# A gated mix of a segment-recurrent transformer and a gated MLP: the MLP branch and the output pass through DRAM scratches in segment and column-block order

## The chip, the cores and the metric

The kernel runs on one core of a Trainium2 chip. Its engines are TensorE (PE; its weight loads are listed as PEld), VectorE (DVE), ScalarE (ACT), GpSimd (POOL) and SyncE (SP). SP computes nothing here; it issues most of the DMAs, one after the other, and waits in its queue until the next one may start. Sixteen DMA engines carry the transfers. The metric is the device time of one execution, in microseconds.

## The reference

Two branches over the same kind of rows are mixed by a gate. Cut to what matters:

```python
# A: 64 segments of 32 rows, 8 memory rows carried from one to the next
for s in range(n_seg):                              # S = 2048 rows, Dm = 640
    h = concat([mem, x[:, 32*s : 32*s+32]], axis=1) # 40 rows
    q, k, v = (einsum('btd,dhe->bhte', h, W) for W in (Wq, Wk, Wv))   # 32 heads of 192
    p = softmax(where(mask, q @ k.T * 192**-0.5, -1e9))
    o = einsum('bhte,hed->btd', p @ v, Wo)
    mem = o[:, :8]; outs.append(o[:, 8:])
a = concat(outs, axis=1)
# B: a gated MLP, 640 -> 1536 -> 640
b = (gelu(x @ w_gate) * (x @ w_up)) @ w_down
g = sigmoid((x * gate_w).sum(-1, keepdims=True))
out = g * a + (1 - g) * b
```

The inputs are bfloat16, and so is the output of 2048 x 640.

## The kernel before

*The MLP first.* `ffn_gu` and `ffn_down` (lines 829 to 880) compute branch B in four blocks of 512 rows. `ffn_down` evacuates 128 rows at a time into a buffer `brow`, and one DMA from ACT's queue stores them into the DRAM tensor `ffn_b_scratch` (`b_scr`, line 878), row by row as the output has them.

*Then the chain of 64 segments* (`segment(s)`, line 1462). The weights Wq, Wk, Wv and Wo don't all fit in SBUF. Most pieces stay there; in each segment 13 pieces of Wq, Wk and Wv (384 KB each) and 3 of Wo (480 KB each) are swapped for their partners as soon as TensorE has used the old piece (`swap_loads`, `load_piece`, line 635). Segments run through the heads forwards and backwards in turn, so that the pieces used last are used first in the next one. What a segment does is a list written out by hand (`PROG`, `PROG1`, `PROG3`): groups of projections `("g", n, k)`, transposes, scores, softmax, `("pv", o)`, the output projection `("wo", o, half)`, and work for later segments (`lf`, `le`, `vb`) that fills TensorE's waits.

*The last 8 rows of a segment, called left rows,* don't feed the next segment's memory. Queries and keys of the left rows of four segments (a group, `g = s // 4`) are computed ahead together, and their output rows are projected with the last segment of the group (`wo_both`).

*The mix.* The output tile of a segment lies in SBUF as four column blocks of 160 on top of each other: partition 32 j + t holds row t, columns 160 j to 160 j + 159. The B rows must lie in the same way. `bz_load(s)` (line 1018) reads the 32 rows of segment s in that form from `ffn_b_scratch`; POOL scales them (`mix1`), DVE adds the gated A rows (`mix2`), and `out_store(s)` (line 1029) writes the tile to the output. The left rows of a group have a tile `bzl` of their own with 32 partitions for each column block, in the order: last segment of the group, then the other three (`LROW = ((3, 4), (0, 3))`). `bzl_load` (line 1024) fills it with eight DMAs, one of 8 and one of 24 rows for each column block; `outl_store` (line 1072) writes it out with eight.

*What sets the order.* Every instruction gets its semaphore waits from the regions that it reads and writes; within an engine, and within SP's queue, the order is the order of the calls. After the MLP all DMAs are issued by SP (`AUXQ = "sp"`, line 908). In a segment SP's queue holds: the K, Q and V pieces, each behind the TensorE instruction that frees its place; `out_store` of the segment before; the next segment's x rows; in the third segment of a group half of `bzl_load`, and in the first half of `outl_store`; the three Wo pieces; `bz_load`; the queries and keys of left rows (`stg_load`) around one more piece; and the other half of `bzl_load` or `outl_store`. The calls stand in the code as follows:

```python
if item == ("g", 1, KT - 1):
    if q:
        out_store(s - 1)
...
if item in (("g", 1, KT - 1), ("pv", NOCT - 2)):
    js = (0, 1) if item[0] == "g" else (2, 3)
    if q == 0 and g > 0:
        outl_store(g - 1, js)
    if q == 2 and g + 1 < NG:
        bzl_load(g, js)
```

*The end.* The last segment and the left rows of the last three are handled apart (`end_load`, `end_store`, line 1065), with six small transfers each from `ffn_b_scratch` and to the output.

Of the kernel before, what the change touches and what calls it, by code (L numbers as in the profile page):

```python
# [6 lines left out]
BF = mybir.dt.bfloat16  # L7
# [231 lines left out]
def _build(nc, A_x, A_mem0, A_Wq, A_Wk, A_Wv, A_Wo, seg_len, w_gate, w_up, w_down,  # L239
           gate_w, out, opts=None):  # L240
    opts = dict(opts or {})
    Bsz, S, Dm = A_x.shape
    M = A_mem0.shape[1]
    H, Dh = A_Wq.shape[1], A_Wq.shape[2]
    Df = w_gate.shape[1]
    L = int(seg_len)
    assert Bsz == 1 and M == 8 and L == 32 and Dh == 192
    assert Dm % 128 == 0 and H % 4 == 0 and S % 128 == 0 and Df % 128 == 0
    KT = Dm // 128
    DJ = Dm // 4  # L250
# [32 lines left out]
    g_scr = nc.dram_tensor("gate_scratch", (M, NSEG), F32, kind="Internal").ap()  # L283
# [163 lines left out]
    LROW = ((3, 4), (0, 3))  # L447
# [403 lines left out]
    def ffn_down(blk):  # L851
        n1 = min(Dm, 512)
        for a in range(FA):
# [14 lines left out]
            bs = a % NBR  # L868
# [18 lines left out]
    for blk in range(NFB):  # L887
        if blk:
            x_stage(blk)
        ffn_gu(blk)  # L890
        if blk == 0:
            chain_init()
        if blk + 1 < NFB:
            ffn_transposes(blk + 1)
        if blk + 2 < NFB:
            ffn_x_load(blk + 2)
        if blk + 1 == NFB:
            load_residents(1, lambda key: key not in loaded.values())
        ffn_down(blk)
        if blk + 2 == NFB:  # L900
            load_residents(1, lambda key: res_off[key] >= ffn_off["xr"] and res_off[key] + piece_size(key) <= ffn_off["xT"])
        if blk == 0:
            x_load(0)
            xl_load(0)
            xl_load(1)
            x_copy(0)
# [108 lines left out]
               name="Kl s%d o%d" % (s, o))  # L1015

    def bz_load(s):
        S_.add(AUXQ, lambda e: e.dma_start(bz, b_scr[L * s:L * s + L, :].rearrange("t (j n) -> j t n", j=4)),
               reads=[Rg("dr", 128 * (s // 4), 128 * (s // 4) + 128)], writes=[r_bz], dma_sem="bz", name="bz load s%d" % s)

    def bzl_load(g, js):
        for j in js:
            for n, (lo, hi) in enumerate(LROW):
                S_.add(AUXQ, lambda e, j=j, n=n, lo=lo, hi=hi: e.dma_start(
                    bzl[32 * j + M * n:32 * j + M * (n + hi - lo)], rows(b_scr, g)[1][lo:hi, :, DJ * j:DJ * (j + 1)]),
                    reads=[Rg("dr", 128 * g, 128 * g + 128)], writes=[r_bzlj[j][n]], dma_sem="bzl%d" % (2 * j + n), name="bzl load g%d" % g)

    def out_store(s):
        S_.add(AUXQ, lambda e: e.dma_start(out2[L * s:L * s + L, :].rearrange("t (j n) -> j t n", j=4), bz),
               reads=[r_bz], writes=[Rg("do%d" % j, s, s + 1) for j in range(4)], dma_sem="outs", watch=True, name="out s%d" % s)  # L1030

    assert r_XLg[1].lo == r_XLg[0].hi and KT * 64 == DJ * 2
    bzx = bview(wsA_off["XLg"], 4 * DJ)
# [4 lines left out]
    r_gx = sreg(wsA_off["xs"], 8)  # L1038

    def end_rows(ap, h, x, lo, hi):  # L1040
        v = ap[L * lo:L * hi, 2 * DJ * h:2 * DJ * (h + 1)]
        return v[0:XA] if x == 0 else v.rearrange("(s t) d -> s t d", t=L)[:, XA:L, :]

    def end_load():
# [21 lines left out]
                   reads=[r_bzx[i]], writes=[Rg("do%d" % (2 * h + t), lo, hi, *((XA, L) if x else (0, XA))) for t in range(2)],  # L1066
                   dma_sem="outx%d" % i, watch=True, name="out end")

    def outl_store(g, js):
        for j in js:  # L1070
            for n, (lo, hi) in enumerate(LROW):
                S_.add(AUXQ, lambda e, j=j, n=n, lo=lo, hi=hi: e.dma_start(
                    rows(out2, g)[1][lo:hi, :, DJ * j:DJ * (j + 1)], bzl[32 * j + M * n:32 * j + M * (n + hi - lo)]),
                    reads=[r_bzlj[j][n]], writes=[Rg("do%d" % j, 4 * g + lo, 4 * g + hi)], dma_sem="outl%d" % (2 * j + n), watch=True, name="outl g%d" % g)

    omg = fview(wsA_off["stats"] + 64, 8)
    r_omg = sreg(wsA_off["stats"] + 64, 8)
# [384 lines left out]
    def segment(s):  # L1462
# [3 lines left out]
        for n, item in enumerate(PROGS[q]):  # L1466
# [210 lines left out]
```

## Time and profile before

| | |
|---|---|
| median of three runs | 1651.54 us (1647.38 to 1653.57) |
| profiled execution, span | 2114.2 us |
| granted TensorE clock in it | 0.654 |
| busy share PE, DVE, ACT, POOL | 99%, 48%, 38%, 26% |
| DMA, mean over the span | 236 GB/s, 499.28 MB in 275415 packets |

The profiled execution is the one that the hardware profiler recorded, from its first to its last instruction; it is longer than the timed runs, and its granted clock stands beside it. A matmul's end is modelled, so a TensorE that is busy all the time need not be at its peak. "SPq" is SP's queue; its instructions take time to issue but aren't counted as busy. A DMA row shows how many transfers of a kind were issued, their size, and the median time from issue to landing where that could be found. The DMA share of a stretch is the mean over sixteen engines.

### The profile page before, as it was taken

What the parts mean: (1) busy time and instruction counts of PE and PEld (TensorE: products, weight loads), DVE (VectorE), ACT (ScalarE), POOL (GpSimd) and SP (SyncE); (2) the same over time, 40 slices, a digit from 0 to 9 for tenths busy, and PEclk for the clock granted to TensorE, in tenths of its full rate; (3) what the DMA queues carried; (4) which work ended last, traced back from release to release, by engine and by line L of the source; (5) the groups of instructions that cost most, each with busy time, mean ns of one, the idle gap of its engine ahead of it and who ended that gap; (6) DMA issues with size and microseconds to landing.
All of it is one profiled execution on the core that took longest, in us unless ns stands there. A gap on an engine that the chain in (4) does not pass through costs nothing.

```text
span 2114.2 us, 75845 instructions
## 1 busy us (share of the span) xinstructions
PE 2098.0 (99%) x37107; PEld 958.1 (45%) x28147; DVE 1005.8 (48%) x3039; ACT 792.9 (38%) x1890; POOL 553.3 (26%) x1625
## 2 busy tenths in 40 slices
PE   9999999999999999999999999999999999999997
PEld 3444344444444444444444444444444444444444
DVE  4233254554545454545545454545455454545453
ACT  1111244343434343444434343434444343434342
POOL 1000023232232223232222323232322223222332
PEclk6666666666666666666666666666666666666666
DMA  9612577776768777677767677776777676777775
GB/s 319 182 33 57 184 268 260 248 270 232 253 219 275 244 258 241 227 255 254 274 233 249 221 268 249 255 251 225 248 256 270 239 258 212 261 256 249 254 264 174
DMA packets 275415, 499.28 MB, mean 236 GB/s; under 512 B 121119, under 2 KB 136327, under 8 KB 275079
## 3 DMA queue, kind: packets, MB, share of 16 engines
q1 hardware_dynamic: 271000, 491.30, 68.8%
q8 instruction: 255, 4.18, 0.8%
q10 hardware_dynamic: 4079, 3.14, 0.5%
q14 instruction: 81, 0.66, 0.1%
HBM read 473.25 MB, written 21.09 MB: 234 GB/s over the span
## 4 chain that ended last, share of the span: by engine, by line
PE 99%; DMA 0%; DVE 0%; SPq 0%; POOL 0%; ACT 0%; issue 0%; ACTq 0%; POOLq 0%; DVEq 0%
PE ps L226 26%; PE ps L1138 25%; PE ps L1338 9%; PE ps L1383 8%; PE ps L1282 4%; PE ps L930 4%; PE ps L839 4%; PE ps L836 4%; PE ps L862 3%; PE ps L1364 3%; PE ps L1187 2%; PE ps L1284 2%; PE ps L234 1%; PE ps L1195 1%; PE ps L971 1%; PE ps L1254 1%
## 5 line engine op out<-in xcount | busy, mean ns | idle before, releaser
L226 PE MATMUL ps<-arena 128*32 128x384 bf16 x8960 | 887.8, 430 | 0.4 <-ACT arena L1159 0.4
L1138 PE MATMUL ps<-arena 128*32 128x384 bf16 x8640 | 857.5, 420 | 2.0 <-DVE arena L1583 2.0
L1138 PEld LDWEIGHTS ps<-arena 128*32 128x32 bf16 x8640 | 303.3, 117 | 525.3 <-issue 379.7
L1176 DVE STREAM_TRANSPOSE arena<-arena 128x384 bf16<-128x384 bf16 x512 | 276.5, 562 | 144.1 <-ACT arena L1159 144.1
L1159 ACT ACTIVATE arena<-ps 128x384 bf16<-128x384 f32 x512 | 230.0, 491 | 160.1 <-PE ps L1138 160.1
L1214 DVE TENSOR_REDUCE arena<-ps 104x4 f32<-104x160 f32 x256 | 83.0, 324 | 340.2 <-PE ps L1202 340.2
L1338 PE MATMUL ps<-arena 128*32 128x320 bf16 x3456 | 241.0, 404 | 0.0
L1012 POOL COPY arena<-arena 128x96 bf16<-128x96 bf16 x256 | 70.2, 274 | 475.3 <-PE ps L1202 311.4
L1267 ACT ACTIVATE arena<-ps 128x448 bf16<-128x448 f32 x192 | 104.4, 544 | 237.7 <-PE ps L1254 233.3
L1179 POOL COPY arena<-arena 64x160 bf16<-64x160 bf16 x256 | 81.9, 320 | 385.5 <-DVE arena L1176 384.3
L1162 ACT ACTIVATE arena<-ps 128x384 bf16<-128x384 f32 x256 | 125.2, 489 | 128.1 <-PE ps L1138 127.5
L1383 PE MATMUL ps<-arena 128*64 128x320 bf16 x1536 | 169.6, 387 | 0.0
L1226 ACT ACTIVATE ps<-ps 104x160 f32<-104x160 f32 x256 | 74.8, 292 | 239.5 <-DVE ps L1216 239.5
L1320 ACT ACTIVATE arena<-ps 128x480 bf16<-128x480 f32 x192 | 109.5, 570 | 93.8 <-PE ps L1284 85.7
L930 PE MATMUL ps<-arena 128*32 128x384 bf16 x1280 | 142.5, 408 | 0.0
L1338 PEld LDWEIGHTS ps<-arena 128*32 128x32 bf16 x3456 | 113.3, 129 | 56.9 <-ACT arena L1261 18.1
L1282 PE MATMUL ps<-arena 128*64 128x160 bf16 x1536 | 135.2, 263 | 0.0
L1284 PE MATMUL ps<-arena 128*64 128x64 bf16 x1536 | 128.6, 225 | 0.0
L1228 DVE TENSOR_REDUCE arena<-ps 104x4 f32<-104x160 f32 x256 | 81.8, 319 | 88.4 <-ACT ps L1226 87.4
L1383 PEld LDWEIGHTS ps<-arena 128*64 128x64 bf16 x1536 | 93.2, 127 | 49.4 <-issue 9.6
L1282 PEld LDWEIGHTS ps<-arena 128*64 128x64 bf16 x1536 | 94.1, 126 | 42.8 <-ACT arena L1159 23.0
L1411 ACT ACTIVATE arena<-ps 128x384 bf16<-128x384 f32 x120 | 57.3, 491 | 123.9 <-DVE arena L1580 74.0
(102 smaller groups left out, 2518.2 us busy)
## 6 DMA issues: line engine op xcount, KB each, us to landing
arena<-in_A_Wk_dram SPq DMA_DIRECT2D x335, 384.0 KB, 5.8
arena<-in_A_Wv_dram SPq DMA_DIRECT2D x335, 384.0 KB, 8.4
arena<-in_A_Wo_dram SPq DMA_DIRECT2D x205, 480.0 KB, 4.3
arena<-in_A_Wq_dram SPq DMA_DIRECT2D x209, 384.0 KB, 4.8
arena<-left_qk_scratch SPq DMA_DIRECT2D x126, 96.0 KB, 3.9
left_qk_scratch<-arena SPq DMA_DIRECT2D x49, 192.0 KB, 4.6
left_qk_scratch<-arena SPq DMA_DIRECT2D x30, 96.0 KB, 3.7
ffn_b_scratch<-arena ACTq DMA_DIRECT2D x16, 160.0 KB, 2.3
```

Source lines behind the costliest of these rows:

```text
L226: return e.add_instruction(mybir.InstMatmult(name=nm, start_tensor_calc=like["start"], stop_tensor_calc=stop, tile_size=(128, 32), tile_po ...
L930: fns.append(lambda e, outp=outp, rhs=rhs, j=j: e.matmul(outp, lhs, rhs, start=(k == 0), stop=(k == KT - 1), tile_position=(0, 32 * j)))
L1138: fns.append(lambda e, outp=outp, rhs=rhs, j=j: e.matmul(outp, lhs, rhs, start=(k == 0), stop=(k == KT - 1), tile_position=(0, 32 * j)))
L1159: S_.add("act", lambda e, m=m, bk=bk: e.activation(out=rows_sb[m], in_=ps[:, bk, 0:384], func=ACTF.Copy), reads=[r_ps[bk]], writes=[r_rows ...
L1162: S_.add("act", lambda e, i=i, bk=bk: e.activation(out=v_sb[i % NVB].rearrange("p (c n) -> p c n", c=3), in_=ps[:, bk, 0:384].rearrange("p ...
L1176: S_.add("dve", lambda e: e.transpose(out=dst[:, :, 0:L], in_=rows_sb[m].rearrange("p (c r) -> p c r", r=L)), reads=[r_rows[m]], writes=[r ...
L1267: S_.add("act", lambda e: e.activation(out=PT, in_=ps[:, bank, 0:PTW + 128], func=ACTF.Copy), reads=[r_ps[bank]], writes=[r_PT], name="pT ...
L1282: return [lambda e: e.matmul(full, v[:, e0:e0 + 64], PTm[:, i], start=True, stop=False, tile_position=(0, 64 * i), skip_group_check=True), ...
L1284: lambda e: e.matmul(part, vl[:, e0:e0 + 64], PTl[:, i], start=False, stop=True, tile_position=(0, 64 * i), skip_group_check=True)]
L1320: S_.add("act", lambda e: e.activation(out=apx(u[:, 0, 0, :], [[rs, na], [3 * rs, 4], [1, R]]), in_=ps[:, A, 0:na * W].rearrange("p (c t r ...
L1338: fns.append(lambda e, i=i, t=t, j=j, gv=gv: e.matmul(ps[32 * j:32 * j + 32, bank, 0:2 * DJ].rearrange("p (h n) -> p h n", h=2), lhs2[i], ...
L1383: S_.add("pe", [lambda e, i=i, g_=g_, c=c, p=p, u=u: e.matmul(ps[64 * i:64 * i + 64, LB, 0:2 * DJ], u[:, c, :], g_[:, c, 2 * DJ * i:2 * DJ ...
```

## The change

Five things are done:

1. The B rows are stored by `ffn_down` into a scratch `b_segments` whose order is segment, column block, row, column. Each 128 rows take four DMAs (one a segment) instead of one; for the last of the four blocks SP issues them instead of ACT. Only the last 128 rows also go to `ffn_b_scratch`, for the end.
2. `bz_load` reads 40 KB that lie in one piece in DRAM, as 128 rows of 160, and `out_store` writes such a piece into a scratch `out_segments` (segments 0 to 59). The last segments still write to the output.
3. The left rows of B are copied, DRAM to DRAM, from `b_segments` into a scratch `b_left` in the order of the tile `bzl` (`b_left_copy`: four during the MLP for the first half of the segments, four during segments 3 to 6 for the second). `bzl_load` and `outl_store` are one DMA each, from `b_left` and to `out_left`.
4. When sixteen segments are finished, the left rows are copied from `out_left` to their places in `out_segments` (`out_left`, four DMAs, one in each of the first four segments after that), and then `out_segments` to the output (`out_copy`, four DMAs, one for each column block, in the four segments that follow). Segments 48 to 59 are copied in segments 61 and 62, four DMAs in each.
5. The places of the calls: `outl_store` stands where its first half stood, `bzl_load` where its second half stood; the copies stand behind `stg_load` in the turn to the next segment.

The diff, without the renamed lines of the end:

```diff
-    b_scr = nc.dram_tensor("ffn_b_scratch", (S, Dm), BF, kind="Internal").ap()
+    b_scr = nc.dram_tensor("ffn_b_scratch", (128, Dm), BF, kind="Internal").ap()
+    b2_scr, o2_scr = [nc.dram_tensor(nm, (NSEG, 4, L, Dm // 4), BF, kind="Internal").ap() for nm in ("b_segments", "out_segments")]
+    b3_scr, o3_scr = [nc.dram_tensor(nm, (NG, 4, 4, M * (Dm // 4)), BF, kind="Internal").ap() for nm in ("b_left", "out_left")]
...
-            S_.add(AUXQ, lambda e, bs=bs, row0=row0: e.dma_start(b_scr[row0:row0 + 128, :], brow[bs]),
-                   reads=[r_brow[bs]], writes=[Rg("dr", row0, row0 + 128)], dma_sem="bw%d" % bs, watch=True,
-                   name="b store %d" % row0)
+            for q in range(4):
+                S_.add("sp" if blk + 1 == NFB else AUXQ, lambda e, bs=bs, row0=row0, q=q: e.dma_start(
+                    b2_scr[row0 // L + q].rearrange("j t n -> t j n"), brow[bs][L * q:L * q + L].rearrange("t (j n) -> t j n", j=4)),
+                    reads=[r_brow[bs]], writes=[Rg("d2", row0 // L + q, row0 // L + q + 1)], dma_sem="bw%d_%d" % (bs, q),
+                    name="b store %d" % row0)
+            if row0 + 128 == S:
+                S_.add("sp", lambda e, bs=bs: e.dma_start(b_scr, brow[bs]), reads=[r_brow[bs]], writes=[Rg("dr", S - 128, S)],
+                       dma_sem="bwl", name="b store")
+
+    def seg_left(scr, lo, hi, q):
+        return scr[lo:hi].rearrange("(g q) j t n -> q g j (t n)", q=4)[q][:, :, XA * DJ:L * DJ]
+
+    def b_left_copy(half, q):
+        g0, g1 = 8 * half, 8 * half + 8
+        S_.add("sp", lambda e: e.dma_start(b3_scr[g0:g1, :, (q + 1) % 4], seg_left(b2_scr, 4 * g0, 4 * g1, q)),
+               reads=[Rg("d2", 4 * g0, 4 * g1)], writes=[Rg("d3", 4 * half + q, 4 * half + q + 1)],
+               dma_sem="bl%d" % q, name="b left copy %d %d" % (half, q))
...
+        if blk == 2:
+            for q in range(4):
+                b_left_copy(0, q)
...
     def bz_load(s):
-        S_.add(AUXQ, lambda e: e.dma_start(bz, b_scr[L * s:L * s + L, :].rearrange("t (j n) -> j t n", j=4)),
-               reads=[Rg("dr", 128 * (s // 4), 128 * (s // 4) + 128)], writes=[r_bz], dma_sem="bz", name="bz load s%d" % s)
-
-    def bzl_load(g, js):
-        for j in js:
-            for n, (lo, hi) in enumerate(LROW):
-                S_.add(AUXQ, lambda e, j=j, n=n, lo=lo, hi=hi: e.dma_start(
-                    bzl[32 * j + M * n:32 * j + M * (n + hi - lo)], rows(b_scr, g)[1][lo:hi, :, DJ * j:DJ * (j + 1)]),
-                    reads=[Rg("dr", 128 * g, 128 * g + 128)], writes=[r_bzlj[j][n]], dma_sem="bzl%d" % (2 * j + n), name="bzl load g%d" % g)
+        S_.add(AUXQ, lambda e: e.dma_start(bz, b2_scr[s].rearrange("j t n -> (j t) n")),
+               reads=[Rg("d2", s, s + 1)], writes=[r_bz], dma_sem="bz", name="bz load s%d" % s)
+
+    def bzl_load(g):
+        S_.add(AUXQ, lambda e: e.dma_start(bzl, b3_scr[g].rearrange("j q (t n) -> (j q t) n", n=DJ)),
+               reads=[Rg("d3", 4 * (g // 8), 4 * (g // 8) + 4)], writes=[r_bzl], dma_sem="bzl", name="bzl load g%d" % g)
 
     def out_store(s):
+        if s < NSEG - 4:
+            S_.add(AUXQ, lambda e: e.dma_start(o2_scr[s].rearrange("j t n -> (j t) n"), bz), reads=[r_bz],
+                   writes=[Rg("o2", s, s + 1)], dma_sem="outs", name="out s%d" % s)
+            return
         S_.add(AUXQ, lambda e: e.dma_start(out2[L * s:L * s + L, :].rearrange("t (j n) -> j t n", j=4), bz),
...
-    def outl_store(g, js):
...
+    def outl_store(g):
+        S_.add(AUXQ, lambda e: e.dma_start(o3_scr[g].rearrange("j q (t n) -> (j q t) n", n=DJ), bzl), reads=[r_bzl],
+               writes=[Rg("o3", g, g + 1)], dma_sem="outl", name="outl g%d" % g)
+
+    def out_left(lo, hi, q):
+        g0, g1 = lo // 4, hi // 4
+        form = "g j x -> g j x" if g1 - g0 == 4 else "g j x -> j g x"
+        S_.add(AUXQ, lambda e: e.dma_start(seg_left(o2_scr, lo, hi, q).rearrange(form), o3_scr[g0:g1, :, (q + 1) % 4].rearrange(form)),
+               reads=[Rg("o3", g0, g1)], writes=[Rg("o2", lo, hi)], dma_sem="outf%d" % q, name="out left s%d" % lo)
+
+    def out_copy(lo, hi, j):
+        form = "s t n -> s t n" if hi - lo == 16 else "s t n -> t s n"
+        S_.add(AUXQ, lambda e: e.dma_start(
+            out2[L * lo:L * hi, DJ * j:DJ * (j + 1)].rearrange("(s t) n -> s t n", t=L).rearrange(form),
+            o2_scr[lo:hi].rearrange("s j t n -> j s t n")[j].rearrange(form)),
+            reads=[Rg("o2", lo, hi)], writes=[Rg("do%d" % j, lo, hi)], dma_sem="outm%d" % j, watch=True, name="out copy s%d" % lo)
...
                     stg_load(s + 1, int(q != 1))
+                if 3 <= s <= 6:
+                    b_left_copy(1, s - 3)
+                lo, i = s // 16 * 16 - 16, s % 16 - 1
+                if lo >= 0 and 0 <= i < 8:
+                    (out_left if i < 4 else out_copy)(lo, lo + 16, i % 4)
+                if s in (NSEG - 3, NSEG - 2):
+                    for i in range(4):
+                        (out_left if s == NSEG - 3 else out_copy)(NSEG - 16, NSEG - 4, i)
...
-            if item in (("g", 1, KT - 1), ("pv", NOCT - 2)):
-                js = (0, 1) if item[0] == "g" else (2, 3)
-                if q == 0 and g > 0:
-                    outl_store(g - 1, js)
-                if q == 2 and g + 1 < NG:
-                    bzl_load(g, js)
+            if item == ("g", 1, KT - 1) and q == 0 and g > 0:
+                outl_store(g - 1)
+            if item == ("pv", NOCT - 2) and q == 2 and g + 1 < NG:
+                bzl_load(g)
```

More of the change, by code (lines that the diff above doesn't have):

```diff
@@ L1017, in bz_load @@
     def bz_load(s):
-        S_.add(AUXQ, lambda e: e.dma_start(bz, b_scr[L * s:L * s + L, :].rearrange("t (j n) -> j t n", j=4)),
-               reads=[Rg("dr", 128 * (s // 4), 128 * (s // 4) + 128)], writes=[r_bz], dma_sem="bz", name="bz load s%d" % s)
-    def bzl_load(g, js):
-        for j in js:
-            for n, (lo, hi) in enumerate(LROW):
-                S_.add(AUXQ, lambda e, j=j, n=n, lo=lo, hi=hi: e.dma_start(
-                    bzl[32 * j + M * n:32 * j + M * (n + hi - lo)], rows(b_scr, g)[1][lo:hi, :, DJ * j:DJ * (j + 1)]),
-                    reads=[Rg("dr", 128 * g, 128 * g + 128)], writes=[r_bzlj[j][n]], dma_sem="bzl%d" % (2 * j + n), name="bzl load g%d" % g)
+        S_.add(AUXQ, lambda e: e.dma_start(bz, b2_scr[s].rearrange("j t n -> (j t) n")),
[3 more added lines that the diff above has]
+               reads=[Rg("d3", 4 * (g // 8), 4 * (g // 8) + 4)], writes=[r_bzl], dma_sem="bzl", name="bzl load g%d" % g)
     def out_store(s):
+        if s < NSEG - 4:
+            S_.add(AUXQ, lambda e: e.dma_start(o2_scr[s].rearrange("j t n -> (j t) n"), bz), reads=[r_bz],
+                   writes=[Rg("o2", s, s + 1)], dma_sem="outs", name="out s%d" % s)
+            return
         S_.add(AUXQ, lambda e: e.dma_start(out2[L * s:L * s + L, :].rearrange("t (j n) -> j t n", j=4), bz),
-               reads=[r_bz], writes=[Rg("do%d" % j, s, s + 1) for j in range(4)], dma_sem="outs", watch=True, name="out s%d" % s)
+               reads=[r_bz], writes=[Rg("do%d" % j, s, s + 1) for j in range(4)], dma_sem="oute", watch=True, name="out s%d" % s)
     assert r_XLg[1].lo == r_XLg[0].hi and KT * 64 == DJ * 2
@@ L1040, in end_rows @@
     def end_rows(ap, h, x, lo, hi):
-        v = ap[L * lo:L * hi, 2 * DJ * h:2 * DJ * (h + 1)]
+        off = S - ap.shape[0]
+        v = ap[L * lo - off:L * hi - off, 2 * DJ * h:2 * DJ * (h + 1)]
         return v[0:XA] if x == 0 else v.rearrange("(s t) d -> s t d", t=L)[:, XA:L, :]
@@ L1067, in end_store @@
                    dma_sem="outx%d" % i, watch=True, name="out end")
-    def outl_store(g, js):
[L1070 to L1074, printed above, removed]
+    def outl_store(g):
[12 more added lines that the diff above has]
+            reads=[Rg("o2", lo, hi)], writes=[Rg("do%d" % j, lo, hi)], dma_sem="outm%d" % j, watch=True, name="out copy s%d" % lo)
     omg = fview(wsA_off["stats"] + 64, 8)
```

## The prediction

> **What bounds the kernel now.** I read first the page's head with the cores' list, then the stages, then the DMA issues, last SP's queue in one segment.
>
> ```profile
> core 0: 2114.2 us, clock 0.654
> ```
>
> ```profile
> PE 2098.0 (99%) x37107; PEld 958.1 (45%) x28147; DVE 1005.8 (48%) x3039; ACT 792.9 (38%) x1890; POOL 553.3 (26%) x1625
> ...
> DMA packets 275415, 499.28 MB, mean 236 GB/s; under 512 B 121119, under 2 KB 136327, under 8 KB 275079
> ...
> q1 hardware_dynamic: 271000, 491.30, 68.8%
> ...
> q10 hardware_dynamic: 4079, 3.14, 0.5%
> ...
> PE 99%; DMA 0%; DVE 0%; SPq 0%; POOL 0%; ACT 0%; issue 0%; ACTq 0%; POOLq 0%; DVEq 0%
> ```
>
> The profiled execution is TensorE alone: 99% busy, 99% of the chain that ended last. If that were all, a change of transfers would be worth nothing. But this execution ran at a granted clock of 0.654 and took 2114.2 us, while the three timed runs have a median of 1651.54, which is 0.781 of it. So the timed runs had a faster TensorE, and what hides behind it in the profile need not be hidden in them. At full clock its work would be 2098.0 x 0.654 = 1372 us; 280 us of the median are then something else. The other reading is that TensorE is still the bound, at a clock of 0.654 / 0.781 = 0.84. The stages decide between them (columns: busy time of PE, PEld, DVE, ACT, POOL with counts, granted clock, DMA share, GB/s):
>
> ```profile
> 0.00:242.40 242.40, 240.38 (x882) 98.46 (x883) 80.42 (x144) 39.24 (x66) 16.65 (x39) 0.66 0.50 145
> 242.40:279.20 36.80, 36.45 (x672) 14.24 (x470) 17.24 (x49) 14.60 (x33) 7.90 (x24) 0.65 0.86 312
> 279.20:2069.10 1789.90, 1787.76 (x34988) 828.87 (x26348) 894.38 (x2800) 727.13 (x1763) 519.56 (x1534) 0.65 0.73 249
> 2069.10:2114.20 45.10, 33.39 (x580) 16.53 (x452) 13.80 (x46) 11.88 (x30) 9.20 (x29) 0.63 0.46 157
> ```
>
> The third row is 62 segments: 28.9 us each, of which the sixteen DMA engines are busy 0.73 x 28.9 = 21.1 us in the mean. TensorE needs 28.8 us at 0.654, so 18.9 at full clock: less than the DMA engines. The other rows at full clock: 159 us (TensorE, first row), 0.86 x 36.8 = 32 (DMA, second), 33.4 x 0.654 + 11.7 idle = 34 (last). Together 225, which leaves (1651.5 - 225) / 62 = 23.0 us for a segment of the timed runs, if they ran at full clock. TensorE's 18.9 doesn't explain that; the DMA mean of 21.1 nearly does.
>
> What is above the mean? The issues (out<-in, engine, count, KB each, median us to landing):
>
> ```profile
> arena<-in_A_Wo_dram SPq DMA_DIRECT2D x205, 480.0 KB, 4.3
> arena<-in_A_Wq_dram SPq DMA_DIRECT2D x209, 384.0 KB, 4.8
> ...
> left_qk_scratch<-arena SPq DMA_DIRECT2D x49, 192.0 KB, 4.6
> left_qk_scratch<-arena SPq DMA_DIRECT2D x30, 96.0 KB, 3.7
> ...
> arena<-ffn_b_scratch SPq DMA_DIRECT2D x63, 40.0 KB
> out_dram<-arena SPq DMA_DIRECT2D x63, 40.0 KB
> ...
> arena<-ffn_b_scratch SPq DMA_DIRECT2D x60, 2.5 KB
> arena<-ffn_b_scratch SPq DMA_DIRECT2D x60, 7.5 KB
> out_dram<-arena SPq DMA_DIRECT2D x60, 2.5 KB
> out_dram<-arena SPq DMA_DIRECT2D x60, 7.5 KB
> ```
>
> The view gives a landing time only where completions of all sixteen engines are found. The rows without one are just those whose pattern's outermost dimension is small: 4 (column blocks) for the 40 KB ones, 8 and 3 for the left rows. I read them as running on 4, 8 and 3 engines.
>
> **The price of a row.** All these transfers move rows of 320 B. The stretch in which only weight loads run gives the rate of an engine:
>
> ```profile
> 870.00:878.00 8.00, 0.65 1.03 409
> ```
>
> 409 / 16 = 25.6 GB/s, so 320 B cost at least 12.5 ns. From the other side, the ACT queue (q10) took 0.5% of 16 x 2114.2 us for 4079 packets of 770 B in the mean, 41 ns each. I take 27 ns, the middle. Rows on the busiest engines in a group of four segments: 4 x 32 (bz load) + 4 x 32 (out store) + left rows, load and store, 2 x (4 x 8 + 4) = 328, that is 82 a segment or 2.2 us; the mean over sixteen engines is 20 rows, 0.54 us. The busiest thus hold 21.1 + 1.7 = 22.8 us of work in a segment, against the 23.0 above. I conclude that the timed runs are held by three or four overloaded DMA engines.
>
> **The change, part by part.** One segment (third of four) of SP's queue:
>
> ```profile
> 899.70 1.38 SPq L635 DMA_DIRECT2D arena<-in_A_Wv_dram  x3
> 901.12 0.60 SPq L1029 DMA_DIRECT2D out_dram<-arena  x1
> 901.76 0.47 SPq L743 DMA_DIRECT2D arena<-x_scratch  x1
> 902.28 2.84 SPq L1024 DMA_DIRECT2D arena<-ffn_b_scratch  x4
> 910.18 2.81 SPq L635 DMA_DIRECT2D arena<-in_A_Wo_dram  x3
> 913.04 0.59 SPq L1018 DMA_DIRECT2D arena<-ffn_b_scratch  x1
> 913.67 0.48 SPq L1005 DMA_DIRECT2D arena<-left_qk_scratch  x1
> 914.67 0.33 SPq L635 DMA_DIRECT2D arena<-in_A_Wq_dram  x1
> 915.04 0.44 SPq L1005 DMA_DIRECT2D arena<-left_qk_scratch  x1
> 915.53 2.38 SPq L1024 DMA_DIRECT2D arena<-ffn_b_scratch  x4
> 920.72 2.11 SPq L635 DMA_DIRECT2D arena<-in_A_Wk_dram  x2
> ```
>
> *Out store, L1029.* 32 rows on four engines become 8 on sixteen: 24 x 27 = 0.65 us less there, 0.22 more elsewhere. It stands between the Wv loads and the Wo loads, which TensorE needs next, so it is on the path.
> *Left rows, L1024 and L1072.* 72 rows a group become 16: 14 a segment, 0.38 us. Half stands ahead of the Wo loads (0.2 us on the path), half in the turn of the segment. SP issues 14 fewer in a group; the four at 902.28 took 2.84 us, but SP then waited until 910.18 for TensorE. At full clock the 9.1 us from 901.12 shrink to 5.9 and SP's issues there take 0.60 + 0.47 + 2.84 = 3.9: still covered, so nothing for it.
> *bz load, L1018.* Also 0.65 us less, but in the turn: from 913.04 to 920.72 SP only waits for TensorE to give the K slots back, 7.7 us, about 5 at full clock. There the queue holds bz, two of L1005, one Wq load (384 KB, 0.96 us at 409 GB/s). It counts where that backlog still stands when the Wk loads come; half of it, 0.3 us.
> *Added: copies of the output inside DRAM.* Every finished sixteen segments get four out_left copies (rows of 2560 B, with the same for the b rows 0.5 row or 0.05 us a segment and engine) and four out_copy of 512 rows of 320 B, so 8 rows a segment and engine, 60 segments. No row shows a DRAM to DRAM transfer. Lower bound 12.5 ns, above; the 512-row stores (L1419, 96 KB, 3.7 us to landing) land no later than the 128-row ones of 192 KB (4.6), so such 32 rows an engine cost under 1 us, 31 ns. I take the dearer 41 ns: 0.33 us a segment. They are issued in the turn, behind the Wq load, four segments in sixteen, 1.3 us each, and wait for stores a segment old. No cover is left there if the engines are the bound, so it counts in full.
> *FFN.* The b rows are stored in four parts by segment. For three blocks ACT issues them; it is busy 39.24 of 242.40 us, so it hides there. In the last block SP issues 16 and one for the end, each behind an evacuation; the resident Wo loads are next in that queue, and five issues of 0.6 us put them 3 us later in a stage bound by DMA: +3 us once.
> *End.* In segment 61 the four last out_left wait for one another, three landings of some 3.7 us (the 96 KB stores' row), 11 us, less the 5 that the turn covers, and the Wk loads stand behind them: +6 us once (0 to 11).
>
> Were every engine's work the whole time, a segment would go from 22.8 to 21.1 - 0.54 + 0.54 + 0.33 + 0.05 = 21.5 us: 1.3 us, 81 us over 62. That is the high end. By the path alone it is 0.65 + 0.2 + 0.3 - 0.38 = 0.77. I take 0.85, nearer the path: 53 us, less 9 once: 1651.5 - 44 = **1607 us**. Against the profile's own time: at 0.654 TensorE covers all of it, and I expect its span within 2100 to 2120 if the clock is the same.
>
> **Rivals.**
> *TensorE bounds the timed runs, at 0.84 (no change).* For it: 1372 / 0.84 + 16 = 1649. Against it: the DMA's 22.8 us would be longer than 18.9 / 0.84 = 22.5, so even then the engines take part. It gives 1645 to 1658.
> [...]
> *Turn-bound (small gain).* If the waits at the turn (last Wo load, sums, K slots, new loads) set the period, only 0.3 us a segment are won: 1651 - 19 + 9 = 1641.
> *Dear copies (slower).* A row read from DRAM and written to DRAM, 320 B at a time into a pitch of 1280 B, may cost far more than a row to or from SBUF. 480 of them lie on every engine; from 41 + 44000 / 480 = 133 ns on, the change loses; at 200 ns it gives 1607 + 480 x 0.159 = 1683. Against it: the 512-row store above.
> [...]
> *It doesn't do what it says.* If the 40 KB transfers ran on sixteen engines already, only the copies remain: 0.38 x 60 + 9 = 32 us more, 1683. The missing landing times speak against it.
>
> **How the numbers follow.** Overloaded engines 0.55 (1565 to 1633), turn-bound 0.15 (1633 to 1643 for the most part), TensorE 0.10, dear copies 0.14, no effect 0.06. About 0.5% (8 us) is what can be told from no change. Faster 0.70, same 0.10, slower 0.20. The range runs from 1562 (the high end of 81 us and no cost of the end) to 1662 (just above the no-change case); it leaves out the slower cases.
>
> **What would show it.** Right: the 40 KB rows and the single left transfer have landing times, four rows of copies appear, and the runs are about 44 us faster though the profiled span hardly moves. Copies: landing near 4 us and a DMA share that rises by about 0.01; near 8 us and more, they are dear. Wrong: no gain with all that in place would mean that the overloaded engines were not the bound; a loss, that the copies or SP's waits in front of the Wk loads are.

## The result, and the profile after

| | median | ratio to before |
|---|---|---|
| before | 1651.54 us (1646.53 to 1659.29, 11 runs) | |
| after | 1663.57 us (1656.38 to 1670.41, 11 runs) | 1.0077 (95%: 1.0057 to 1.0098) |

The change costs 12.7 us (0.0077 x 1651.5). Forecast were 1607 us, in a range of 1562 to 1662. The profiled execution of after ran at a clock of 0.994; so the kernel before was profiled once more, and that execution ran at 0.995. These two can be compared row by row, which the record at 0.654 didn't allow; they differ by 9.1 us. First the cores' list and rows 1 and 3 of the page, for before:

```profile
core 0: 1652.2 us, clock 0.995
...
PE 1565.1 (95%) x37090; PEld 776.7 (47%) x28147; DVE 997.8 (60%) x3039; ACT 784.5 (47%) x1890; POOL 549.6 (33%) x1625
...
q1 hardware_dynamic: 271000, 491.30, 84.8%
```

and for after:

```profile
core 0: 1661.3 us, clock 0.994
...
PE 1570.3 (95%) x37107; PEld 774.2 (47%) x28147; DVE 999.9 (60%) x3039; ACT 785.2 (47%) x1890; POOL 551.9 (33%) x1625
...
q1 hardware_dynamic: 282644, 495.85, 85.7%
```

TensorE is busy 95% of either span, and SP's queue q1 puts 0.857 x 1661.3 - 0.848 x 1652.2 = 23 us more work on each DMA engine. Now the stages. I cut them at the end of the MLP and at two starts of POOL's copy of the next segment's x rows (line 811 before, 813 after), which comes once a segment; between its starts for segments 1 and 63 lie 62 segments. Columns as in the prediction. Before:

```profile
0.00:168.00 168.00, 162.16 (x870) 78.90 (x887) 82.37 (x144) 39.12 (x66) 16.22 (x39) 0.99 0.71 209
168.00:195.60 27.60, 25.94 (x673) 11.52 (x472) 17.09 (x49) 14.52 (x32) 7.85 (x24) 1.00 0.97 357
195.60:1612.00 1416.40, 1351.24 (x34988) 671.88 (x26348) 884.35 (x2800) 719.05 (x1763) 516.39 (x1533) 1.00 0.89 316
1612.00:1652.20 40.20, 25.72 (x580) 14.40 (x451) 14.02 (x48) 11.77 (x30) 9.18 (x29) 0.87 0.50 180
```

After, with a fifth row for the last of the 62:

```profile
0.00:170.40 170.40, 163.58 (x887) 78.17 (x887) 82.49 (x144) 38.92 (x66) 15.84 (x39) 1.00 0.74 207
170.40:201.30 30.90, 27.56 (x666) 11.51 (x458) 17.31 (x49) 14.67 (x33) 7.93 (x25) 0.94 0.86 307
201.30:1622.00 1420.70, 1354.08 (x34992) 670.27 (x26358) 886.43 (x2801) 719.85 (x1763) 518.88 (x1534) 1.00 0.90 317
1622.00:1661.30 39.30, 25.08 (x580) 14.22 (x448) 13.64 (x46) 11.71 (x30) 9.21 (x29) 0.91 0.58 195
1592.40:1622.00 29.60, 21.92 (x508) 9.59 (x380) 12.81 (x42) 10.20 (x26) 8.01 (x25) 0.88 0.75 261
```

A segment takes 1416.40 / 62 = 22.84 us before and 1420.70 / 62 = 22.91 after; without the last one 1391.1 / 61 = 22.80. So the segments gain next to nothing, and the loss sits in two places: the MLP and what follows it up to segment 1 (2.4 + 3.3 us), and one segment near the end, 29.6 us instead of 23.1 (1612.0 - 1588.9, POOL's last two of these copies before). It runs from the copy for segment 62 to that for 63; the transfers that delay it are issued in segment 61, and the texts below call it segment 61.

The DMA issues of after show that the change does what it says:

```profile
arena<-b_segments SPq DMA_DIRECT2D x63, 40.0 KB, 4.6
out_segments<-arena SPq DMA_DIRECT2D x60, 40.0 KB, 9.1
...
out_dram<-out_segments SPq DMA_DIRECT2D x12, 160.0 KB, 4.4
...
arena<-b_left SPq DMA_DIRECT2D x15, 40.0 KB, 3.3
out_left<-arena SPq DMA_DIRECT2D x15, 40.0 KB, 8.6
...
out_segments<-out_left SPq DMA_DIRECT2D x12, 40.0 KB
```

The 40 KB transfers between SBUF and the scratches now have landing times, which the view gives only where it finds sixteen completions for each. The 63 loads from `b_segments` have 1008 in the trace; the 63 from `ffn_b_scratch` before had 315, five each. The copies to the output land in 4.4 us. The copies of left rows (last line) have no landing time and five completions each, so by the prediction's reading they still run on fewer engines. "On four engines" is that reading in the texts below too: no trace here names the engine that a row ran on.

### The profile page after: what moved, and what is told of

Same layout as the page of the kernel before. It is cut to its first block, busy times and chain, and to the rows that moved or that the text cites. A ratio compares the mean times of both kernels' runs of the same rounds, so it can differ in the third digit from the quotient of the medians.

```text
span 1661.3 us, 75708 instructions
## 1 busy us (share of the span) xinstructions
PE 1570.3 (95%) x37107; PEld 774.2 (47%) x28147; DVE 999.9 (60%) x3039; ACT 785.2 (47%) x1890; POOL 551.9 (33%) x1625
## 3 DMA queue, kind: packets, MB, share of 16 engines
q10 hardware_dynamic: 8687, 2.49, 0.7%
## 5 line engine op out<-in xcount | busy, mean ns | idle before, releaser
L1169 PE MATMUL ps<-arena 128*32 128x384 bf16 x8640 | 642.7, 329 | 19.9 <-DMA arena<-in_A_Wv_dram 7.8
L226 PE MATMUL ps<-arena 128*32 128x384 bf16 x8960 | 646.8, 327 | 5.0 <-DMA arena<-in_A_Wq_dram 1.2
L1169 PEld LDWEIGHTS ps<-arena 128*32 128x32 bf16 x8640 | 227.2, 96 | 396.1 <-issue 263.4
L1369 PE MATMUL ps<-arena 128*32 128x320 bf16 x3456 | 184.1, 301 | 12.0 <-issue 6.8
L1031 POOL COPY arena<-arena 128x96 bf16<-128x96 bf16 x256 | 69.6, 272 | 246.2 <-PE ps L1233 158.2
L1313 PE MATMUL ps<-arena 128*64 128x160 bf16 x1536 | 118.1, 240 | 5.8 <-ACT arena L1190 3.4
L1414 PE MATMUL ps<-arena 128*64 128x320 bf16 x1536 | 122.3, 304 | 0.9 <-DMA arena<-in_A_Wo_dram 0.6
L1369 PEld LDWEIGHTS ps<-arena 128*32 128x32 bf16 x3456 | 88.2, 96 | 54.7 <-ACT arena L1292 18.6
L949 PE MATMUL ps<-arena 128*32 128x384 bf16 x1280 | 108.9, 329 | 0.9 <-issue 0.9
L1315 PE MATMUL ps<-arena 128*64 128x64 bf16 x1536 | 104.1, 193 | 1.3 <-issue 1.3
L1359 POOL COPY arena<-arena 128x96 bf16<-128x96 bf16 x192 | 51.7, 269 | 160.6 <-ACT arena L1341 93.8
L1313 PEld LDWEIGHTS ps<-arena 128*64 128x64 bf16 x1536 | 81.7, 109 | 41.2 <-ACT arena L1193 14.4
```

Of the source, the lines that this page charges most:

```text
L226: return e.add_instruction(mybir.InstMatmult(name=nm, start_tensor_calc=like["start"], stop_tensor_calc=stop, tile_size=(128, 32), tile_po ...
L949: fns.append(lambda e, outp=outp, rhs=rhs, j=j: e.matmul(outp, lhs, rhs, start=(k == 0), stop=(k == KT - 1), tile_position=(0, 32 * j)))
L1169: fns.append(lambda e, outp=outp, rhs=rhs, j=j: e.matmul(outp, lhs, rhs, start=(k == 0), stop=(k == KT - 1), tile_position=(0, 32 * j)))
L1313: return [lambda e: e.matmul(full, v[:, e0:e0 + 64], PTm[:, i], start=True, stop=False, tile_position=(0, 64 * i), skip_group_check=True), ...
L1315: lambda e: e.matmul(part, vl[:, e0:e0 + 64], PTl[:, i], start=False, stop=True, tile_position=(0, 64 * i), skip_group_check=True)]
L1369: fns.append(lambda e, i=i, t=t, j=j, gv=gv: e.matmul(ps[32 * j:32 * j + 32, bank, 0:2 * DJ].rearrange("p (h n) -> p h n", h=2), lhs2[i], ...
```

## The experiments

Effects in microseconds are (ratio - 1) x 1651.5, and each trace is of one execution. Theory 1 and 2 are those of the expectations.

**The kernel before once more** (no edit).

> The kernel before, unchanged, for a profile at the clock of the timed runs. Theory 1 (the overloaded engines never set the pace; the change only pays waits at single places, at the end of the MLP and in segment 61): segments of 22.9 us as in the changed kernel, within 0.1, and segment 61 near 22 us instead of 29.6. Theory 2 (the spreading gains, but the copies inside DRAM cost more): segments of 22.7, of equal length in every block of sixteen, while those of the changed kernel are longer where copies are issued.

Median 1648.89 us, ratio 0.9991 (0.996 to 1.0023). The profiled execution took 1653.96 us at a clock of 0.995; its rows stand above. TensorE is busy 1351.24 / 62 = 21.8 us in a segment of 22.84. That is theory 1, but for the 23.1 us of segment 61.

**Three parts of the change.** Without the copies of finished segments (the output of segments 0 to 59 then stays in the scratch):

```diff
-                if lo >= 0 and 0 <= i < 8:
-                    (out_left if i < 4 else out_copy)(lo, lo + 16, i % 4)
-                if s in (NSEG - 3, NSEG - 2):
...
```

> The changed kernel without out_left and out_copy: segments 0 to 59 never reach the output, which is left out here. Theory 1: only the wait in segment 61 goes, about 7 us, so 1656. Theory 2: the copies' whole price goes and the gain of the sixteen engines is seen: 1620 to 1635.

Only the way of the B rows (items 1, half of 2 and half of 3 of the change), with `out_store` and `outl_store` as before:

```diff
     def out_store(s):
-        if s < NSEG - 4:
-            S_.add(AUXQ, lambda e: e.dma_start(o2_scr[s].rearrange("j t n -> (j t) n"), bz), reads=[r_bz],
...
```

> The kernel before with the change's B side alone (b_segments, b_left, bz load and left B rows in one transfer each on sixteen engines); out stores as before. Theory 1: the end of the MLP costs a few us and the segments don't change: 1652 to 1658. Theory 2: the bz load and the left rows gain a part of what I forecast and there are no output copies: 1625 to 1640.

And only the way of the output, with `ffn_b_scratch`, `bz_load` and `bzl_load` as before:

```diff
+        if s < NSEG - 4:
+            S_.add(AUXQ, lambda e: e.dma_start(o2_scr[s].rearrange("j t n -> (j t) n"), bz), reads=[r_bz],
...
```

> The kernel before with the change's output side alone (out_segments, out_left, the copies); the B rows as before. Theory 1: segment 61 costs about 7 us: 1656 to 1660. Theory 2: the copies cost more than the store gains: 1660 to 1675.

Ratios 1.0039 (1.0015 to 1.0063), 1.0024 (0.9995 to 1.0052) and 1.0092 (1.006 to 1.0125): 6.4, 4.0 and 15.2 us. No part gains, though each spreads rows that four engines had. The two halves together come to 19 us against 12.7; their intervals are 5 us to either side, so the sum says no more than that both belong to the loss. Theory 2, that spread gains are eaten by the copies, falls for the whole change: without the copies there is still no gain. But the output side alone costs what theory 2 gave it (1660 to 1675). In its trace the 61 segments up to the delayed one take 1402.5 us, 9 more than the 1393.3 before, and TensorE waits 8.7 us for the Wk loads where it waited 1.5; why, no run settles.

**No swaps: what can a DMA relief win at all?** All piece loads within the segments are left out (the wrong weights lie in those places).

```diff
-            load_piece(other, "swap s%d" % seg)
+            loaded[slot_id[other]] = other
```

> The kernel before without the swaps of weight pieces during the segments (left out: the partner pieces are never loaded, so the heads concerned use the wrong weights). It gives the pace of TensorE and the other engines alone. If TensorE's own pace is the bound, as its 95% busy share says: segments of 21.8 us or a little less, 1585 to 1645. If the loads set the pace, with TensorE's stalls hidden inside the modelled ends of its matmuls: segments near 19 to 20 us, 1430 to 1500.

1587.26 us, ratio 0.9608 (0.9581 to 0.9634). Its stage of 62 segments:

```profile
195.80:1557.00 1361.20, 1333.70 (x34992) 668.59 (x26347) 883.50 (x2801) 720.00 (x1763) 516.39 (x1533) 1.00 0.11 27
```

The DMA share falls from 0.89 to 0.11, and a segment still takes 21.96 us, TensorE busy 98% of it. All sixteen swaps together cost a segment 0.88 us, 55 us over the 62; with the stretch behind them (29.7 us instead of 40.2) it is the 65 us of the ratio. A gain of 53 us in the segments by spreading a few rows would have been nearly all of these 55.

**No output** (segments 0 to 59 and the left rows aren't stored): the relief of the output's four-engine rows without any price.

```diff
     def out_store(s):
+        if s < NSEG - 4:
+            return
...
     def outl_store(g, js):
+        return
```

> The kernel before without out stores of segments 0 to 59 and without stores of left rows (left out: those output rows). The four engines lose 0.65 to 1 us a segment and nothing is added. If they set the pace: 1651 - 62 x 0.8 = 1600. If not: 1645 to 1652.

Ratio 0.9977 (0.9959 to 0.9995): 3.8 us. That is the worth of 32 rows in each segment on four engines, and of the left rows.

**More on four engines, more on sixteen.** Three extra stores of 32 KB behind `out_store`, once as 4 x 32 rows on four engines, once as 128 rows on sixteen:

```diff
+        for x in range(3):
+            S_.add(AUXQ, lambda e, x=x: e.dma_start(dum[s, x].rearrange("t (j n) -> j t n", j=4), ident), reads=[r_ident], dma_sem="dum%d" % x, watch=True, name="extra s%d" % s)
```

> The kernel before with three more stores a segment from a constant tile (4 x 32 rows of 256 B each, in the pattern of the out store, so on four engines) to a scratch that nobody reads, right behind the out store. That puts 96 rows, some 1.9 us a segment, on four engines. If the four engines set the pace, as I forecast: 1651 + 62 x 1.9 = 1770. If they have slack of 1 us or more: 1651 to 1690.

```diff
+            S_.add(AUXQ, lambda e, x=x: e.dma_start(dum[s, x], ident), reads=[r_ident], dma_sem="dum%d" % x, watch=True, name="extra s%d" % s)
```

> The same three extra stores of the same bytes as 128 rows each, on sixteen engines: 24 rows, 0.5 us a segment, on every engine. If the four engines set the pace: 1651 + 62 x 0.5 = 1682, far below the four-engine form. If what counts is the mean of all engines: the same 1682, but the four-engine form no slower than this. If neither counts: 1650 to 1660 for both.

Ratios 1.1093 (1.106 to 1.1125) and 1.0172 (1.0143 to 1.0201): 181 us and 28 us. The form on sixteen engines costs about what its rows take there by the expectation's estimate (0.5 x 62 = 31 us). The form on four lies above both of its expectations, and above the work that it adds: 96 rows at the 18.3 ns that they took in its trace are 1.8 us a segment, 109 us in all. Its granted clock was lower too, 0.959, and no run says what part of the 181 us that is. So more rows on four engines can be very dear, while relief of them is worth 4 us. The two don't lie on one line; the next runs ask why.

**One extra store on four engines**, the same edit with `range(1)`:

> The kernel before with one extra store of 4 x 32 rows of 256 B in each segment, on four engines, 32 rows or 0.59 us on each of them by the 18.3 ns of the run with three. If the four engines of the kernel before lie just below another engine that ends last, and only what exceeds it counts (a kink): at most 15 us more, 1652 to 1667. If each row on the four engines counts from the first on (a third of the run with three): 40 to 60 us more, 1691 to 1712.

Ratio 1.0165 (1.0138 to 1.0192): 27 us. Neither bound of the expectation held, neither 15 nor 40. The trace tells more than the time. SP's queue in one segment of this kernel (start, duration, instruction):

```profile
902.37 2.40 SPq L636 DMA_DIRECT2D arena<-in_A_Wv_dram  x5
904.81 0.61 SPq L1030 DMA_DIRECT2D out_dram<-arena  x1
905.46 0.56 SPq L1033 DMA_DIRECT2D extra_scratch<-arena  x1
906.06 3.44 SPq L744 DMA_DIRECT2D arena<-x_scratch  x1
909.55 1.54 SPq L636 DMA_DIRECT2D arena<-in_A_Wo_dram  x3
```

and of the kernel before:

```profile
887.05 2.35 SPq L635 DMA_DIRECT2D arena<-in_A_Wv_dram  x5
889.45 0.60 SPq L1029 DMA_DIRECT2D out_dram<-arena  x1
890.08 0.47 SPq L743 DMA_DIRECT2D arena<-x_scratch  x1
894.12 1.54 SPq L635 DMA_DIRECT2D arena<-in_A_Wo_dram  x3
```

The issue of the x rows, an instruction that waits for no semaphore in the trace, takes 3.44 us instead of 0.47: SP is held up while two four-engine transfers stand behind five V loads. Over the 61 issues between 195 and 1610 us its median is 2.74 us, with 46 above 1 us. The Wo loads stand behind it, and TensorE waits for them (line waited for, total, times, longest), 23.1 us against 4.7 before. In the run with three extra stores the median is 2.40 us, and the same wait 107.6 us. With one extra store:

```profile
PE ps L1367 <- DMA arena<-in_A_Wo_dram: 23.1, 27, 2.7
```

and before:

```profile
PE ps L1364 <- DMA arena<-in_A_Wo_dram: 4.7, 12, 0.9
```

**The same rows past SP's queue.** ACT issues the extra store, on four engines or, as a control, on sixteen:

```diff
-            S_.add(AUXQ, lambda e, x=x: e.dma_start(dum[s, x].rearrange("t (j n) -> j t n", j=4), ident), reads=[r_ident], dma_sem="dum%d" % x, watch=True, name="extra s%d" % s)
+            S_.add("act", lambda e, x=x: e.dma_start(dum[s, x].rearrange("t (j n) -> j t n", j=4), ident), reads=[r_ident], dma_sem="dum%d" % x, watch=True, name="extra s%d" % s)
```

> The kernel before with one extra store of 4 x 32 rows of 256 B in each segment on four engines, as in the run with one extra store (27 us more), but issued by ACT in place of SP. If the work on the four engines is what costs (the prediction's premise): again 20 to 30 us more, 1669 to 1681. If SP held up at its next issue is what costs: at most 10 us more, below 1662, and SP's issue of the x rows stays near 0.5 us.

> The same extra store from ACT's queue, the same 32 KB, but as 128 rows spread over sixteen engines (8 rows, 0.15 us on each). It is the price of ACT's issue and of the bytes. Either theory: 0 to 8 us more. Where it costs as much as the one on four engines, that one's price is ACT's issue and not the engines.

Ratios 1.0033 (1.001 to 1.0056) and 1.0016 (0.9994 to 1.0038): 5.5 and 2.6 us, and with four engines the issue of the x rows is back at a median of 0.53 us and the wait for the Wo loads at 6.4 us. The same 32 rows, again on four engines, cost 27 us in SP's queue and no measurable amount beyond their bytes in ACT's. So the work of the four engines, of which this adds 0.59 us a segment or 37 us in all (32 rows at 18.3 ns, an estimate), is not what sets the pace. It was 5.5 us where the rows had a queue of their own, 27 us where weight loads stood behind them in one. Whether the loads' place behind the rows or SP's delay makes the difference, these runs don't show, as both go away in the same step.

**The extra store moved** in SP's queue, in among the K loads at the front of the segment:

```diff
+    def extra_store(s):
...
                 if s and q == 0:
                     out_store(s - 1)
+                if s:
+                    extra_store(s - 1)
```

> The extra store on four engines issued by SP again, but moved to the front of the segment, among the K loads, away from the store of the output in three segments of four. If the work on the four engines costs: again 20 to 30 us more. If SP held up by two four-engine transfers close together behind the V loads costs: 10 us more at most, and no issue on SP's queue with a median above 1 us.

Ratio 1.01 (1.0067 to 1.0133): 16.5 us, between the two expectations. No issue on SP has a median above 1 us any more, so SP held up isn't the whole price. TensorE waits longer for the loads behind the rows all the same: 6.0 us for Wk, 8.6 for Wv and 10.1 for Wo, against 1.5, 4.4 and 4.7 before. How the 27 us divide between the two stays open.

**One swap less**: the last Wv piece is never loaded (its heads compute with what lies there).

```diff
+            if other[0] == 2 and other[2] == KT - 1:
+                loaded[slot_id[other]] = other
+                continue
             load_piece(other, "swap s%d" % seg)
```

> The kernel before without one of the sixteen swaps: the last piece of Wv isn't loaded, so its heads compute with the weights that lie there. 0.97 us less on each of the sixteen engines in a segment. If the work of all sixteen engines paces part of the segment: up to 50 us less, 1595 to 1635 (the kernel without any swaps took 1587, which is the floor). If TensorE alone and the waits at the turn pace it: above 1645.

Ratio 0.9856 (0.9832 to 0.988): 24 us, of 60 us of work (0.97 x 62, by the expectation's estimate) taken off every engine. So taking work off all sixteen engines does count, here at 0.4 of its size. This piece is also one that TensorE waits for, and how much of the 24 us is that one load's, no run separates.

**The delay in segment 61.** SP's queue in after, where the four copies of left rows of segments 48 to 59 are issued:

```profile
1592.54 1.03 SPq L637 DMA_DIRECT2D arena<-in_A_Wq_dram  x1
1593.61 0.44 SPq L1024 DMA_DIRECT2D arena<-left_qk_scratch  x1
1594.09 8.45 SPq L1097 DMA_DIRECT2D out_segments<-out_left  x4
1602.58 0.45 SPq L1024 DMA_DIRECT2D arena<-left_qk_scratch  x1
1603.08 2.58 SPq L637 DMA_DIRECT2D arena<-in_A_Wk_dram  x2
```

Each waits for the one before, as they claim to write the same rows. In the next kernel each names its own quarter:

```diff
-               reads=[Rg("o3", g0, g1)], writes=[Rg("o2", lo, hi)], dma_sem="outf%d" % q, name="out left s%d" % lo)
+               reads=[Rg("o3", g0, g1)], writes=[Rg("o2", lo, hi, 32 * q, 32 * q + 32)], dma_sem="outf%d" % q, name="out left s%d" % lo)
```

> The changed kernel with one thing altered: in segment 61 the four copies of left rows (out_left) note the quarter of out_segments that each writes, so that they no longer wait for one another. Theory 1 (single delays: TensorE's wait in segment 61 comes from this chain, and stands for 7 of the 9 us that the change costs): segment 61 falls from 29.6 us to about 23 and the time by about 7 us, to 1655 to 1658. Theory 2 (the 7 us come from the eight copies' own work on the DMA engines there): segment 61 stays above 28 us and the time at 1660 or more.

```profile
1594.84 2.49 SPq L1097 DMA_DIRECT2D out_segments<-out_left  x4
1597.38 0.45 SPq L1024 DMA_DIRECT2D arena<-left_qk_scratch  x1
1598.56 0.83 SPq L637 DMA_DIRECT2D arena<-in_A_Wk_dram  x2
```

8.45 us become 2.49, the K loads follow 4.5 us earlier, and the segment takes 22.0 us instead of 29.6. Ratio 1.005 (1.0032 to 1.0068): 8.3 us, 4.5 less than the whole change. Theory 2 falls by the segment; of the time, 7 us were expected, and the intervals are 3 us to either side.

**The delay behind the MLP.** In addition ACT issues the B stores of the last block:

```diff
-                S_.add("sp" if blk + 1 == NFB else AUXQ, lambda e, bs=bs, row0=row0, q=q: e.dma_start(
+                S_.add(AUXQ, lambda e, bs=bs, row0=row0, q=q: e.dma_start(
```

> As the run with the quarters noted, and the B rows of the last block of the MLP are issued by ACT in place of SP, so that the resident Wo loads are queued on SP before the MLP ends, as in the kernel before. Theory 1 (the rest of the loss lies between the MLP's end and segment 1): another 3 to 5 us, 1650 to 1654, level with the kernel before, and no better: with both delays away the relief of the four engines is worth nothing that can be measured. Theory 2 (the relief has a worth that the delays hid): clearly below 1648.

Ratio 1.0023 (1.0003 to 1.0042), 3.8 us: 4.5 less than the last run, as expected, but that run's interval doesn't exclude it, and the place that I had named was not mended: the x copy for segment 1 starts at 199.4 us instead of 199.6, against 195.6 before. The same with the copies of finished segments left out as well:

> The changed kernel without the copies of finished segments (the output of segments 0 to 59 is left in the scratch and never reaches the output tensor), and with the B rows of the last MLP block issued by ACT. All reliefs of the four engines are in place, none of the added work at the end. Theory 1 (the relief is worth nothing measurable): 1646 to 1653, within 0.4% of the kernel before. Theory 2 (the relief has a worth that the copies and delays eat up): below 1643.

Ratio 1.0014 (0.9989 to 1.0039), x copy at 200.8 us. So I moved the stores of all four blocks, and the one for the end, to POOL, which waits 30 us for the end of the MLP in any case (copies and mended quarters kept):

```diff
-                S_.add(AUXQ, lambda e, bs=bs, row0=row0, q=q: e.dma_start(
+                S_.add("pool", lambda e, bs=bs, row0=row0, q=q: e.dma_start(
```

> As the run with both delays mended, but POOL issues the stores of the B rows in all four blocks of the MLP; POOL waits 30 us for the MLP's end in every trace. If the issues on SP's or ACT's queue make the chain start late: the x copy for segment 1 at 194 to 197 us and the time 3 to 4 us below the run with ACT, ratio to the kernel before 0.998 to 1.001. If the stores themselves (320 B rows into the DRAM scratch, beside the weight loads) make it late: 199 us or later, ratio 1.001 to 1.005.

1652.67 us, ratio 1.0001 (0.9983 to 1.002); the x copy starts at 196.4 us, so it is the issues on SP's or ACT's queue that made it late. SP's queue in after, in the run with POOL, and before:

```profile
158.19 0.91 SPq L637 DMA_DIRECT2D arena<-in_A_Wo_dram  x2
161.75 11.54 SPq L881 DMA_DIRECT2D b_segments<-arena  x16
...
175.00 3.57 SPq L637 DMA_DIRECT2D arena<-in_A_Wo_dram  x5
178.62 3.15 SPq L960 DMA_DIRECT2D left_qk_scratch<-arena  x4
```

```profile
168.71 2.65 SPq L637 DMA_DIRECT2D arena<-in_A_Wo_dram  x5
172.15 5.95 SPq L960 DMA_DIRECT2D left_qk_scratch<-arena  x4
```

```profile
168.14 2.35 SPq L635 DMA_DIRECT2D arena<-in_A_Wo_dram  x5
171.56 6.01 SPq L941 DMA_DIRECT2D left_qk_scratch<-arena  x4
```

In after sixteen issues, each behind an evacuation, stand in front of the Wo loads, which go out 6.3 us later than with POOL. With ACT as the issuer these loads were early (169.92 us), but the evacuated left queries and keys weren't stored until 175.99. On either busy queue four issues for one delay something; on POOL's idle queue 0.8 us of the 5.7 are left. The times alone (1.0023 with ACT, 1.0001 with POOL) don't separate the two, as their intervals overlap. With both delays away, and all of the added work in place, the change costs nothing and wins nothing that can be measured, 3 us to either side. No version of the change beats the kernel before.

## Why the prediction was wrong

**What bounds the kernel: the step that failed.** The prediction took TensorE's busy time at a clock of 0.654 times 0.654: 18.9 us a segment at full clock. Measured are 21.8. The costliest and a small matmul, at 0.654 (the record that the prediction read; columns of part 5: busy, mean ns | idle before):

```profile
L226 PE MATMUL ps<-arena 128*32 128x384 bf16 x8960 | 887.8, 430 | 0.4 <-ACT arena L1159 0.4
...
L1284 PE MATMUL ps<-arena 128*64 128x64 bf16 x1536 | 128.6, 225 | 0.0
```

and at 0.995:

```profile
L226 PE MATMUL ps<-arena 128*32 128x384 bf16 x8960 | 645.0, 326 | 4.2 <-ACT arena L1159 1.0 <-issue 0.5
...
L1284 PE MATMUL ps<-arena 128*64 128x64 bf16 x1536 | 104.2, 193 | 1.7 <-issue 1.5
```

430 ns became 326 (0.76), 225 became 193 (0.86); 0.654 / 0.995 = 0.66 was expected. As matmuls overlap (8960 of 430 ns are more than the 887.8 us of the first line), the busy time says more: 0.73 and 0.81 for these lines, 1351.24 / 1787.76 = 0.756 for all of TensorE over the 62 segments. So part of a matmul's time doesn't go with the granted clock. Ends are modelled, so waits hidden in the later rows aren't excluded; but with nearly no transfers (no swaps) TensorE is busy 1333.70 / 62 = 21.5 us all the same. With 18.9 too low, 4.1 of the 23.0 us of a segment seemed to be something else, and 22.8 us of work on four engines seemed to explain it. In truth 1.0 us was left over, and that fit was chance. The 23.0 itself was good (22.84). The 22.8 was a little high: at this clock the mean is 0.89 x 22.84 = 20.3 us, and 62 rows more at 24 ns (the mean of the 40704 packets of 320 B in SP's queue of after, for which 27 was taken) make 21.8, by estimate.

**The change, part by part.**
- *Output store, left rows, bz load: 53 us by 0.85 a segment.* Mis-sized by nearly all of it: segments 22.84 before and 22.80 after without the delayed one, 2 us over 62; 3.8 us for the output's part where nothing stands against it. The 81 us named as the high end lie above the 65 us that all swaps cost together. The four engines' rows don't set the pace, as the run with ACT showed.
- *Copies: 0.33 us a segment at 41 ns a row, 20 us in all.* They cost nothing measurable: with ACT as the issuer the ratio is 1.0023 with them (quarters noted) and 1.0014 without, which is 1.5 us, 5 to either side. The run with POOL has them all too, at 1.0001. Landing near 4 us and a DMA share higher by 0.01 (0.89 to 0.90) came as named.
- *MLP: +3 us, behind SP's issues.* Right in place, low in size: the x copy for segment 1 is 5.7 us late, and POOL's queue takes all but 0.8 of that away. That ACT's issues hide in the first three blocks was wrong: a Wo load that waits for the third block goes out at 130.50 us in after, 128.79 before and 129.01 with POOL, and with ACT for all four blocks 3.8 us are left.
- *End: +6 us.* Right: 29.6 us against 22.0 once the chain is gone.

**The rivals.** "TensorE bounds the timed runs" was right in its first half, at full clock and not at 0.84; it had 0.10 because the 18.9 spoke against it. It holds 21.96 of 22.84 us. "Turn-bound" still expected 19 us from the relief, and "dear copies" and "doesn't do what it says" fall by the rows above. The sign came from single delays (rightly named, 9 us forecast) with no gain to pay for them, a case that had no chance of its own.

The expected profiled span at the old clock can't be judged, since that clock didn't come back.

## What to carry to other kernels

If a profile ran at a lower clock than the timed runs, don't scale busy time by the clock (here 0.756 measured, 0.66 by the clocks): take a profile at the clock of the timed runs, or leave the bound open. Ask first what the whole resource can give (here a run without swaps: 65 us), before sharing a gain out over its parts. A split of one DMA into four costs issue time on its queue (here a median of 0.43 us for each of the sixteen B stores on SP), so put the issues where the engine is idle (POOL left 0.8 us of a delay of 5.7), and look what stands behind them.

## What the runs showed of the hardware

- One core alone was profiled at a granted clock of 0.654 once, and at 0.959 to 0.999 in all later profiles of this case. TensorE's busy time over 62 segments at 0.995 was 0.756 of that at 0.654; the clocks alone give 0.66.
- The issue of a DMA on SP can itself be held up, with no semaphore wait in the trace: 2.74 us in the median instead of 0.47, when two transfers of 4 x 32 rows, each on four engines, had gone into the same queue behind five weight loads.
- The same 32 rows on four engines cost 27 us, 16.5 us or 5.5 us over 62 segments, by queue and place in it.
